# Chunked recurrent attention with a routed feed-forward: the chunk loop written out as one list, the triangular inverse taken in two halves, copies cut to their live columns

## The chip, the cores and the metric

One core of a Trainium2 chip runs the whole program. The metric is the device time in microseconds (us) of one execution; lower is better. The kernel before was run three times.

The core has a tensor engine (PE, with its weight loads shown as PEld), a vector engine (DVE), a scalar engine (ACT), GpSimd (POOL) and a queue engine (SP) that here only issues DMAs. Each takes its instructions in the order in which they were written into its queue, and waits at an instruction until the semaphores that it names are there.

## The reference, cut to what matters

```
B, H, S, D = 4, 8, 768, 40                       # r, k, v, w, a, b: each [B, H, S, D]
for t in range(S):
    y[:, :, t] = einsum('bhd,bhde->bhe', rt, state)
    Sa = einsum('bhde,bhe->bhd', state, at)
    state = state * wt[:, :, None, :] - einsum('bhd,bhe->bhde', Sa, bt) + einsum('bhd,bhe->bhde', vt, kt)

x = y.transpose(0, 2, 1, 3).reshape(3072, 320)
logits = x @ w_gate                              # [320, 8]: one of 8 experts for each token
gate_w = softmax(logits)[expert_idx]             # expert_idx = argmax
out[mask_e] = gate_w * (relu(x[mask_e] @ w1[e]) @ w2[e])      # w1 [320, 1024], w2 [1024, 320]
```

So there are 32 independent recurrences (4 batches by 8 heads) of 768 steps on a 40x40 state, then a feed-forward in which each of 3072 tokens goes through one expert.

## The kernel before

**Attention.** The 768 steps are cut into 24 chunks of 32 (`NC`, `C`). In one chunk the 32 recurrences are handled together, as four groups of eight (two "types" `ty` by two halves `j`), one group to a quarter of the 128 partitions. A chunk c goes through these stages, named by the letters that the issue order uses:

- *preparation*, up to nine chunks ahead: loads of the chunk's W, KB and A; `scan` (running product of w, DVE, L224); `inv` (1/product as Ln and Exp, ACT, L229 and L230); `gmul` (one Newton step for the reciprocal, two DVE operations, L241 and L242); `kbmul` and `qmul` (two products over 128x1024 elements, on POOL in the loop, L235 and L246);
- *E* (`estage`): 16 products on PE for the chunk's four 32x32 triangular blocks per recurrence; `m2` copies one part into `M2c`, `m1` the other back into Q (ACT, L263, L275, L276), and `m1_mask` masks it on POOL (L281);
- *inversion* (`tops`), once for a group of four chunks: 128 triangular 32x32 matrices, one to a partition, are inverted by back substitution on DVE. `step(j)` for j = 30 to 1 is a product (L301) and a subtraction (L303) on j x (31-j) elements. The first group alone does it in halves: `step2(j)` for j = 14 to 1 (L309, L311) inverts the two 16x16 diagonal blocks at once;
- `tbd`: four copies on ACT (L331) set the chunk's inverses into a block-diagonal 128x128 tile `TBD`; in the first group the corner between the two halves is made by two sets of PE products (L337, L347) instead;
- the recurrence: *R* (`rhs`, 32 PE products per chunk, one ACT copy), *U* (`ustage`, 32 products with `TBD`, four ACT copies into `SVS`), *S* (`sstage`, 32 products, then four DVE products, L408, which give the state `SVR` of the next chunk). R of the next chunk waits for them;
- beside it *T* (`sT`), *u* (`ut`), *K* (`kbt`): transposes on PE, copied by ACT; *A* (`astage`, masked by DVE, L444) and *y* (`ystage`, L463 on PE, L469 on DVE): the output;
- every second chunk *r* (`route_a`) and *b* (`route_b`): the gate, the token's expert and its row, and two indirect DMAs by POOL (L538) that scatter 128 rows each to `Xs` in memory.

One fp32 PE product is two rows of the profile, except for transposes.

**Order.** Up to chunk 4 the order is a hand-written list (`START`), kept as written on all five engines. From there on a chunk's stages are *written* in the order of the string `ORDER`, with shares of `tops` between them, and the framework's scheduler places them on the engines. Beside the stages the kernel issues products on constant data only to keep the tensor engine's clock up (`w` in `START`, and `busy`).

**Feed-forward** (`moe`). Each expert gathers its rows from `Xs` (L830), splits them and its weights into a high and a low half, and multiplies high by high, high by low and low by high: `l1` (L877 to L882), `l2` (L897 to L905), then a scaled copy and an indirect DMA to the output (L911). `check` and three operations at the end (L954 to L956) verify that w lies in a range; a product at the very end (L1065) turns that into a flag that every engine reads.

Of the kernel before, what the change touches and what calls it, by code (L numbers as in the profile page):

```python
# [42 lines left out]
START = ("W0 s0 l0 j0 W1 s1 a1 a0 w22 c0 k1 w12 l1 g0 Q0 g1 W2 s2 l2 q1 W3 s3 w9 c5 g2 a2 q2 l3 e0 w3 n0 e1 k2 w1 W4 "  # L43
# [18 lines left out]
NKB, NG = 9, 10  # L62


def prepare(inputs):
# [7 lines left out]
    W = np.zeros((NC, 80, 16, C + 1), f32)  # L73
    W[..., 1:] = em(w)
# [4 lines left out]
    VR[..., 0:40], VR[..., 64:104] = V[..., 0::2, :], V[..., 1::2, :]  # L79
# [36 lines left out]
    d["cq"] = np.broadcast_to((ii[None] == (jj % C)[:, None])[:, None, 0:16], (128, 8, 16)).astype(f32)  # L116
# [7 lines left out]
def attention(tc, nc, d, ctx, Xs, okt, sent):  # L124
# [963 lines left out]
```

## Time and profile before

| | us |
|---|---|
| three runs | 706.08, 705.46, 701.49; median 705.46 |
| the profiled execution: its time | 701.49 |
| its span, first to last instruction | 701.5 |
| first state product of the loop (L408) | starts at 71.9 |
| last state product (L408) | starts at 432.7 |
| first gather of the feed-forward | starts at 459.0 |
| busy in the span: PE, DVE, ACT, POOL | 601.3, 535.8, 422.9, 228.7 |

The profiled execution is the fastest of the three, 0.6% under the median. All times in a profile are counted from the span's start. A group's row gives its count, its busy time, the mean of one instruction in nanoseconds, and the idle time of the engine just before. PEclk is the share of its full clock that the tensor engine was granted.

### The profile page before, as it was taken

How to read it: one execution, taken by the hardware profiler on the slowest of the kernel's cores; microseconds unless marked ns; L12 is line 12 of the kernel's file. 1: busy time of each engine (PE TensorE's matmuls, PEld its weight loads, DVE VectorE, ACT ScalarE, POOL GpSimd, SP SyncE). 2: the span in 40 equal slices, each digit the busy share in tenths (PEclk: the TensorE clock that was granted, in tenths of full speed). 3: DMA queues.
4: the chain of work that ended last, by engine and by line, in shares of the span. 5: the costliest groups of instructions: out<-in, count | busy, mean ns of one | idle time of the engine just before them, and what ended most of it. 6: DMA issues, size and time to landing. Idle time of an engine off the chain costs nothing. (4 is left out here: it accounts for less than half of the span.)

```text
span 701.5 us, 25718 instructions
## 1 busy us (share of the span) xinstructions
PE 601.3 (86%) x10942; PEld 510.3 (73%) x10942; DVE 535.8 (76%) x1074; ACT 422.9 (60%) x962; POOL 228.7 (33%) x239
## 2 busy tenths in 40 slices
PE   7477786877978877868889899889999999999994
PEld 3345565766867676757778788758898898988984
DVE  7999699998999999999789634558657576485531
ACT  2565755678759867978786887445535445355320
POOL 5860534546545544457312101200111101201101
PEclk9788767897877788888889989869999999999998
DMA  6484457253434343424224332886454464552100
GB/s 200 119 210 121 141 180 254 75 161 111 123 103 121 103 122 103 133 90 129 78 82 128 111 93 82 243 245 212 134 174 127 145 220 129 168 189 74 56 1 31
DMA packets 48207, 93.26 MB, mean 133 GB/s; under 512 B 11577, under 2 KB 28090, under 8 KB 48024
## 3 DMA queue, kind: packets, MB, share of 16 engines
q1 hardware_dynamic: 45528, 83.65, 39.9%
q0 software_dynamic: 2560, 7.92, 3.2%
q8 instruction: 88, 1.44, 0.9%
q14 instruction: 31, 0.25, 0.1%
HBM read 78.98 MB, written 13.21 MB: 131 GB/s over the span
## 5 line engine op out<-in xcount | busy, mean ns | idle before, releaser
L911 POOL DMA_INDIRECT out<-yo,tok x32 | 30.8, 964 | 207.6 <-DVE yo L910 149.8
L301 DVE TENSOR_TENSOR tmp<-Mt,Tt 128x30 f32<-128x30 f32 (+9 forms) x150 | 79.7, 532 | 2.8
L303 DVE TENSOR_TENSOR Tt<-Tt,tmp 128x30 f32<-128x30 f32 (+9 forms) x150 | 77.1, 514 | 3.2
L886 DVE SCALAR_TENSOR_TENSOR hx<-m_hp,hx 128x384 fp32r<-128x384 f32 (+1 forms) x128 | 41.0, 383 | 34.9 <-ACT hx L884 34.9
L246 POOL TENSOR_TENSOR Q<-AT,G 128x1024 f32<-128x1024 f32 x18 | 50.3, 2796 | 40.9 <-DVE G L242 14.0
L884 ACT ACTIVATE hx<-m_hp 128x448 fp32r<-128x448 f32 x64 | 31.4, 543 | 49.0 <-PE m_hp L882 44.8
L897 PE MATMUL m_yp<-w2h,hx 128*128 128x320 f32 x192 | 61.0, 317 | 0.0
L899 PE MATMUL m_yp<-w2h,hx 128*128 128x320 f32 x192 | 59.1, 308 | 0.0
L898 PE MATMUL m_yp<-w2l,hx 128*128 128x320 f32 x192 | 59.1, 308 | 0.0
L402 PE MATMUL ps_r<-SVS,KS 128*40 128x40 f32 x1472 | 49.8, 228 | 9.3 <-ACT SVS L390 6.2
L364 ACT COPY KS<-ps_g 64x416 f32<-64x416 f32 x96 | 48.1, 501 | 14.8 <-PE ps_g L360 10.0
L281 POOL TENSOR_SCALAR_AFFINE_SELECT Q<-Q 32x512 f32<-32x512 f32 x44 | 38.1, 865 | 57.4 <-ACT Q L275 50.1
L255 PE MATMUL ps_g<-Q,KB 128*64 128x64 f32 x768 | 38.4, 273 | 20.9 <-POOL Q L246 10.5
L463 PE MATMUL psY<-Y,KS 128*40 128x32 f32 x1504 | 50.4, 221 | 5.2 <-DVE Y L444 4.3
L402 PEld LDWEIGHTS ps_r<-SVS,KS 128*40 128x40 f32 x1472 | 44.1, 141 | 12.3 <-ACT SVS L390 8.6
L255 PEld LDWEIGHTS ps_g<-Q,KB 128*64 128x64 f32 x768 | 34.4, 183 | 25.5 <-POOL Q L246 11.9
L331 ACT COPY TBD<-Tc 32x256 f32<-32x256 f32 x80 | 50.8, 635 | 3.2 <-DVE Tc L314 1.3
L463 PEld LDWEIGHTS psY<-Y,KS 128*40 128x40 f32 x1504 | 44.9, 142 | 10.0 <-DVE Y L444 6.7
L408 DVE TENSOR_TENSOR SVR<-ps_r,F 40x320 f32<-40x320 f32 x92 | 44.9, 488 | 8.8 <-PE ps_r L402 6.2
L877 PE MATMUL m_hp<-x,w1h 128*128 128x448 f32 x128 | 50.1, 391 | 0.4 <-ACT x L860 0.4
L538 POOL DMA_INDIRECT Xs<-xr,si x24 | 27.9, 1164 | 61.5 <-ACT TBD L331 15.9
L878 PE MATMUL m_hp<-x,w1h 128*128 128x448 f32 x128 | 47.7, 373 | 0.0
(187 smaller groups left out, 1555.2 us busy)
## 6 DMA issues: line engine op xcount, KB each, us to landing
w2r<-in_w SPq DMA_DIRECT2D x8, 1280.0 KB
w1r<-in_w SPq DMA_DIRECT2D x8, 1024.0 KB
VU<-in_VT SPq DMA_DIRECT2D x48, 160.0 KB
SVR<-in_VR SPq DMA_DIRECT2D x48, 104.0 KB
SVS<-in_VS SPq DMA_DIRECT2D x24, 208.0 KB
KB<-in_KB SPq DMA_DIRECT2D x30, 160.0 KB
KB<-in_KBP SPq DMA_DIRECT2D x9, 512.0 KB
Xs<-xr SPq DMA_DIRECT2D x7, 648.0 KB
```

The source lines that it names most:

```text
L246: eng.tensor_tensor(at(Q, s), buf(s)[3], g, ALU.mult)
L255: TE.matmul(e[j][:, x], kb[:, p, :], q[:, :, p, :], start=True, stop=True, tile_position=(0, 64 * j))
L301: V.tensor_tensor(t, Mt[:, 0:j, j:j + 1].broadcast_to([128, j, n]), Tt[:, j:j + 1, j + 1:32].broadcast_to([128, j, n]), ALU.mult)
L303: V.tensor_tensor(Tt[:, 0:j, j + 1:32], Tt[:, 0:j, j + 1:32], t, ALU.subtract)
L331: A.copy(o[bb:bb + 32, :, bb:bb + 32], t[bb:bb + 32, :, n0:n0 + 8].rearrange("p i n->p n i"))
L364: A.copy(ks[0:64, u * 8 + z:u * 8 + 8:2], ts[u][64 * z:64 * z + 64])
L402: TE.matmul(s[TR[ty], x], ks[:, p, o:o + 40], sv[:, p, o:o + 40], start=True, stop=True, tile_position=(0, o))
L463: TE.matmul(py[TR[ty], p], ks[:, p, o:o + 40], y2[:, ty, p, :], start=True, stop=True, tile_position=(0, o))
L877: TE.matmul(hp, w1h[:, k, s], xh[:, k], start=k == 0, stop=False)
L897: TE.matmul(yp, hh[:, ft, qs], w2h[:, ft], start=ft == 0, stop=False)
L898: TE.matmul(yp, hh[:, ft, qs], w2l[:, ft], start=False, stop=False)
L899: TE.matmul(yp, hl[:, ft, qs], w2h[:, ft], start=False, stop=ft == 7)
```

## The change

**Order.** `ORDER` becomes one list of some 700 words for the whole loop, chunk 0 to 23, kept as written on all five engines: a word names a stage and its chunk, and each time it comes the stage's next part is issued; `t` is one step of the inversion, `f` two products on constant data ("filler pair", twelve in all). `START` is shorter. The products of `YW` before y go, except for the last chunk; `w` in `START` falls from 140 to 85.

**Inversion.** All six groups do the 14 steps on two 16x16 halves; `step` works in place on `Tt` (no `Mt`, no mask product; POOL zeroes the half that isn't wanted with memsets, L300 to L303). `merge` makes the corner for every chunk: 32 products on 32x32 tiles, four copies, 16 products of two heads on 64x64 tiles, one copy. `TBD` and its copies go: U reads the inverses from `Tc` directly.

**Preparation.** `inv` and `gmul` go. Instead a reciprocal of 16 columns and a second scan, running backwards, give 1/product. `kbmul` and `qmul` run on DVE for all chunks.

**Recurrence and copies.** R takes both types in one product: 16 products on 64 columns by 80 instead of 32 on 32 columns by 40; its copy is 128x640 instead of 128x320. S ends in two DVE products on 40x640 instead of four on 40x320. The copies of K leave out 24 of 104 columns.

**Scatters and end.** The four scatters of two routings no longer wait for each other; nor do those of the output. In the feed-forward `x3` and its copy go (the low half of w1's last 64 rows is multiplied with both halves of x), the last expert does its short block before its last full one, and the flag is made before that block.

```diff
-ORDER = ".05 R A T U b E .2 S .2 y C u K r .5 p 2 B"
+ORDER = ("y0 B0 B1 B0 M3 B0 j4 q4 i0 A0 B1 K0 B0 U0 B1 U0 S0 u0 p5 p5 S0 M2 p6 p6 K0 i1 E5 B2 u0 B1 T1 E5 p7 R1 p7 p8  "
...
+         "R23 u22 R23 r22 r20 U23 A23 A23 T23 U23 u23 y23 r22 T23 u23 y23 ")
+TAIL = "R A T U b E S y u K r"
-YW = tuple((c < 16) + (c == NC - 1) + 5 * (c in (5, 11, 17)) for c in range(NC))
+YW = tuple(int(c == NC - 1) for c in range(NC))
     def scan(s):
-        w, f = buf(s)[:2]
-        V.tensor_tensor_scan(f.rearrange("p a b->p (a b)"), w.rearrange("p a b->p (a b)"), scn,
-                             0.0, ALU.mult, ALU.max)
-    def inv(s):
-        _, f, nt, _ = buf(s)
-        A.activation(nt, f[:, :, 1:], AF.Ln)
-        A.activation(nt, nt, AF.Exp, scale=-1.0)
+        w, f, _ = buf(s)
+        back = lambda x: bass.AP(x.tensor, x.offset + 528, [x.ap[0], [-1, 528]])
+        V.tensor_tensor_scan(f.rearrange("p a b->p (a b)"), w[:, 0:528], scn, 0.0, ALU.mult, ALU.max)
+        V.reciprocal(RC[:, 33:WN:33], f[:, :, 32])
+        V.tensor_tensor_scan(back(at(G, s)), back(w), back(RC), 0.0, ALU.mult, ALU.max)
-    def gmul(s):
-        V.tensor_tensor(g, f[:, :, 1:], nt, ALU.mult)
-        V.scalar_tensor_tensor(g, g, 2.0, nt, ALU.subtract, ALU.mult, reverse0=True)
     def tops(k):
         def first():
-            V.transpose(flat(Mt), M2c[0].rearrange("p n t->p t n"))
+            V.transpose(flat(Tt), M2c[0].rearrange("p n t->p t n"))
+            A.copy(at(ML, k)[:, 0:32], M2c[0][:, :, 0:16])
+            G_.memset(Tt[:, 0:16, 16:32], 0.0)
+            for h in (16, 8, 4, 2, 1):
+                G_.memset(bass.AP(Tt.tensor, Tt[:, h, 0:1].offset, [Tt.ap[0], [66 * h, 16 // h], [32, h], [1, h]]), 0.0)
+            G_.memset(flat(Tt)[:, 0:1024:33], -1.0)
-        def step(j):
-            n = 31 - j
-            t = tmp[:, :j * n].rearrange("p (a b)->p a b", b=n)
+        def step(j):
             n = 15 - j
             t = tmp[:, :2 * j * n].rearrange("p (h a b)->p h a b", a=j, b=n)
+    def merge(c):
...
+        q = g4([128, 8, 32])
+                TE.matmul(q[b, x], m[b, (n0 + x) * 16:(n0 + x) * 16 + 32], Tc2[b, :, h:h + 2].rearrange("p a n->p n a"),
+        for b in quads:
+            A.copy(Q1[b, :, o:o + 16].rearrange("p (h l) a->p h l a", l=2), mine(q[b], 16))
+        z = g4([128, 8, 64])
+            for b in (slice(0, 64), slice(64, 128)):
+                TE.matmul(z[b, x], Q1[b, x], t[b, h:h + 2].rearrange("p n a->p (n a)"), start=True, stop=True,
+        A.copy(t[:, n0:n0 + 8, 0:16].rearrange("p (h l) a->p h l a", l=2), mine(z, 32))
     def rhs(c):
-                TE.matmul(r[32 * bb:32 * bb + 32, h], q[:, ty, p, :], sr[:, ty, p // 2, p % 2 * 64:p % 2 * 64 + 40],
-        A.copy(rs, r)
+                TE.matmul(psS[64 * j:64 * j + 64, h, 0:80], q[:, p].rearrange("e t i->e (t i)"),
+                          sr[:, :, h, j * 64:j * 64 + 40], start=True, stop=True, tile_position=(0, 64 * j))
+        A.copy(rs, psS[:, :, 0:80])
     def ustage(c):
-                TE.matmul(u[bb:bb + 32, h], tb[:, h, bb:bb + 32], rs[:, h, :],
-                          start=True, stop=True, tile_position=(0, bb))
+                TE.matmul(u[bb:bb + 32, h], t[bb:bb + 32, c % 4 * 8 + h, :], rs[bb:bb + 32, h, bb // 32 % 2 * 40:bb // 32 % 2 * 40 + 40],
+                          start=True, stop=True, tile_position=(bb, bb))
+    def step_prep(s):
+            scan(s)
+                load_w(s + 1)
+            kbmul(s, V)
+            qmul(s, V)
+                load_a(s + 1)
```

The first place is DVE's queue near the end of an inversion. In the kernel before (`Mt`, `Tt`, `tmp` are the inversion's tiles, L532 belongs to the routing, L444 to A, L314 is the transposition that ends it):

```order
L301 TENSOR_TENSOR tmp<-Mt,Tt 128x108
L444 TENSOR_TENSOR Y_104<-ps_g,mask 64x2x256 x2
L532 RECIPROCAL xr<-gt 128x2
L303 TENSOR_TENSOR Tt<-Tt,tmp 128x4x27
L301 TENSOR_TENSOR tmp<-Mt,Tt 128x84
L303 TENSOR_TENSOR Tt<-Tt,tmp 128x3x28
L301 TENSOR_TENSOR tmp<-Mt,Tt 128x58
L303 TENSOR_TENSOR Tt<-Tt,tmp 128x2x29
L301 TENSOR_TENSOR tmp<-Mt,Tt 128x30
L303 TENSOR_TENSOR Tt<-Tt,tmp 128x30
L314 STREAM_TRANSPOSE Tc<-Tt 128x1024
```

In the changed kernel, at the start of the third group's inversion (L244 and L246 are the two scans of a preparation, the scans being printed under the name of a related operation; L253 and L258 its two products; L310 and L312 an inversion step; L397 the state products):

```order
L244 SCALAR_TENSOR_TENSOR FF<-Wt,scn 128x528
L245 RECIPROCAL RC<-FF 128x16
L246 SCALAR_TENSOR_TENSOR G_91<-Wt,RC 128x528
L310 TENSOR_TENSOR tmp<-Tt 128x28
L312 TENSOR_TENSOR Tt<-Tt,tmp 128x2x14
L253 TENSOR_TENSOR KB_87<-KB_87,FF 128x1024
L258 TENSOR_TENSOR Q_88<-AT,G_91 128x1024
L310 TENSOR_TENSOR tmp<-Tt 128x52
L312 TENSOR_TENSOR Tt<-Tt,tmp 128x2x13x2
L397 TENSOR_TENSOR SVR<-psS,F_113 40x8x2x40 x2
```

Thirty pairs to a group have become fourteen, and the preparation's two big products stand among them on the same engine.

The second place is POOL's queue in the middle of the loop. Before (L246 and L235 are the big products, L236 the small copy of the scan's last column, L281 the masks, L538 the scatters, L514 the token numbers):

```order
L246 TENSOR_TENSOR Q_76<-AT,G_93 128x1024
L538 DMA Xs<-xr,si 3584x324
L235 TENSOR_TENSOR KB_77<-KB_77,FF 128x1024
L236 COPY F_112<-FF 128x16
L281 AFFINE_SELECT Q_76<-Q_76 32x512 x2
L514 COPY xr<-cg 128x2
```

And in the changed kernel (L302 and L303 clear parts of the inversion's tile, L254 is the small copy, L293 the masks, L530 the scatters):

```order
L302 MEMSET Tt 128x16
L303 MEMSET Tt 128x32
L254 COPY F_113<-FF 128x16 x2
L503 COPY gt<-cg 128x8
L504 TENSOR_TENSOR gt<-cg,gt 128x8
L505 TENSOR_TENSOR cg<-gt 128x8
L506 COPY xr<-cg 128x2
L507 MEMSET xr 128x2x2
L293 AFFINE_SELECT Q_76<-Q_76 32x16x32 x2
L530 DMA Xs<-xr,si 3584x324 x2
```

The big products are gone from POOL; small copies, masks, memsets and scatters remain.

The third place is PE's queue over about one chunk late in the loop. Before, from R to S (L375 is R, L441 A, L415 T, L385 U, L463 y, L255 E, L402 S; six constant products of L448 stand ahead of L463 and are printed here with their first pair only):

```order
L375 MATMUL ps_r<-SVR,Q_86 32x40 x32
L441 MATMUL ps_g<-RT,VU 64x2x32 x16
L415 MATMUL ps_g<-ident,SVR 104x40 x16
L385 MATMUL ps_r<-rs,TBD 32x40 x32
L448 LDWEIGHTS scn
L448 MATMUL psY<-scn 128x512
```

And in the changed kernel from one S to the next (L392 S, L414 u, L343 the corner's second set, L355 K, L430 A, L368 R, L404 T, L378 U, L472 the gate, L447 y):

```order
L392 MATMUL psS<-SVS,KS_123 40x40 x32
L414 MATMUL ps_g<-ident,SVS 104x32 x16
L343 MATMUL ps_g<-Tc_116,NB 64x64 x16
L355 MATMUL ps_g<-ident,KB_89 128x104 x8
L430 MATMUL ps_g<-RT,VU 64x2x32 x16
L368 MATMUL psS<-SVR,Q_90 64x80 x16
L404 MATMUL ps_g<-ident,SVR 104x40 x16
L378 MATMUL psU<-RS,Tc_116 32x40 x32
L472 MATMUL ps_g<-xT,wg 32x128 x8
L447 MATMUL psY<-Y_105,KS_123 40x32 x32
L355 MATMUL ps_g<-ident,KB_73 128x104 x8
L392 MATMUL psS<-SVS,KS_123 40x40 x32
```

R has half as many rows, each wider, and the corner's two sets (L332, elsewhere, and L343) now run in every chunk.

More of the change, by code (lines that the diff above doesn't have):

```diff
@@ L315, in last @@
-            if k < 1:
-                V.transpose(flat(Tc2), Tt.rearrange("p a b->p b a")[:, 16:32])
-        o = [(1.2, first), (1.2, second)]
-        for j in range(14 if k < 1 else 30, 0, -1):
-            if k < 1:
-                o.append((2 * (0.075 + 2 * j * (15 - j) / 960), lambda j=j: step2(j)))
-            else:
-                o.append((2 * (0.075 + j * (31 - j) / 960), lambda j=j: step(j)))
-        o.append((1.2, last))
-        return o
-    def tbd(c):
-        t, n0, o = Tc[0], (c % 4) * 8, at(TBD, c)
-        if c >= 4:
-            for bb in range(0, 128, 32):
-                A.copy(o[bb:bb + 32, :, bb:bb + 32], t[bb:bb + 32, :, n0:n0 + 8].rearrange("p i n->p n i"))
-            return
+            V.transpose(flat(Tc2), Tt.rearrange("p a b->p b a")[:, 16:32])
@@ L333, in tbd, with mine @@
+            V.transpose(at(Tc, k).rearrange("p n a->p a n"), flat(Tt))
+        return [(2, first)] + [(2 * (0.12 + 2 * j * (15 - j) / 960), lambda j=j: step(j)) for j in range(14, 0, -1)] + [
+            (3.1, last)]
+    def mine(x, w):
+        return bass.AP(x.tensor, x.offset, [x.ap[0], [4 * w, 4], [3 * w, 2], [1, 16]])
+    def merge(c):
+        t, m, n0 = at(Tc, c // 4), flat(at(ML, c // 4)), c % 4 * 8
         quads = [slice(bb, bb + 32) for bb in range(0, 128, 32)]
-        q = g4([128, 8, 16])
+        q = g4([128, 8, 32])
@@ L348, in tbd @@
                           tile_position=(b.start, b.start))
         yield
-        for b in quads:
-            A.copy(o[b, :, b.start:b.start + 16], z[b])
+        A.copy(t[:, n0:n0 + 8, 0:16].rearrange("p (h l) a->p h l a", l=2), mine(z, 32))
     def kbt(c):
@@ L596, in step_u, with step_e @@
             yield from ustage(i)
[L598 to L605 removed]
+    def step_e(s):
         if s < NC:
@@ L777, in attention @@
-    for _ in step_route_b(NC):
-        pass
-    for i in range(1, 4):
-        for j in range(i + 1, 5):
-            tc.declare_no_dep(sent[-i].ins, sent[-j].ins, reason="they write different rows")
-        tc.add_manual_dep(sent[-i].ins, sent[-5].ins.name, mybir.DependencyInfo(
-            mybir.DependencyClass.Sync, mybir.DependencyReason.DATA))
+                    for t in ML:
+                        G_.memset(flat(t)[:, 512:544], 0.0)
+                    DMA.dma_start(Q1, d["cq"])
+    once = {"j": lambda s: kbmul(s, V), "q": lambda s: qmul(s, V), "M": m1_mask}
@@ new lines, in attention @@
+    groups, to, gens = iter(range(1, NC // 4)), [], {}
+    for op in ORDER.split():
+        if op == "t":
+            if not to:
+                to = tops(next(groups))
+            to.pop(0)[1]()
+            continue
+        if op == "f":
+            hot = g4([128, 512])
+            for _ in range(2):
+                TE.matmul(hot, scn[:, 0:128], scn[:, 0:512], start=True, stop=True)
+            continue
+        if op[0] in once:
+            once[op[0]](int(op[1:]))
+            continue
+        if op not in gens:
+            gens[op] = steps[op[0]](int(op[1:]))
+        next(gens[op], None)
@@ new lines, in attention @@
+    gens = {}
+    manual.__exit__(None, None, None)
+    for i in (NC, NC + 1):
+        with tc.manual_schedule(engines={mybir.EngineType.PE}):
+            for step in TAIL.split():
+                if step == "b":
+                    for _ in gens.pop("r", ()):
+                        pass
+                elif step == "r" and i == NC:
+                    gens["r"] = step_route(i)
+                    for _ in range(3):
+                        next(gens["r"])
+                elif step != "r":
+                    for _ in steps[step](i):
+                        pass
@@ L785, in attention @@
+    for g in range(0, len(sent), 4):
+        for i in range(g, g + 4):
+            for j in range(g, i):
+                tc.declare_no_dep(sent[i].ins, sent[j].ins, reason="they write different rows")
+            for j in range(max(g - 4, 0), g) if i > g else ():
+                tc.add_manual_dep(sent[i].ins, sent[j].ins.name, mybir.DependencyInfo(
+                    mybir.DependencyClass.Sync, mybir.DependencyReason.DATA))
     cnt, oh = g4([128, 8]), held["oh"]
```

334 lines of the change are left out of this document (131 added, 203 removed), and 30 rows, old and new, of tables (ORDER, START).

## The prediction

> **What bounds the kernel now.** I read the busy time by stage first, then the starts of one operation that comes once a chunk, then the groups by shape, then the timeline. The stretches show (columns: PE, PEld, DVE, ACT, POOL busy us with counts, granted clock, DMA share, GB/s):
>
> ```profile
> 160.00:200.00 40.00, 31.44 (x819) 27.17 (x817) 37.27 (x73) 30.75 (x73) 22.26 (x21) 0.80 0.38 116
> 240.00:280.00 40.00, 30.38 (x880) 27.53 (x869) 37.63 (x81) 28.87 (x69) 19.35 (x22) 0.82 0.39 114
> 371.00:396.00 25.00, 23.71 (x781) 20.54 (x776) 21.84 (x65) 18.25 (x44) 3.89 (x10) 1.00 0.37 112
> 490.00:694.00 204.00, 201.75 (x1178) 178.66 (x1176) 122.78 (x262) 84.91 (x183) 29.62 (x31) 1.00 0.39 126
> ```
>
> In the middle of the loop DVE is busy 93% of the time and PE 78%: DVE bounds it. Late (371 to 396), when preparations have run out, PE is busy 95%. From 490 on PE is full and nothing here changes its work. The span splits at four events:
>
> ```profile
> L408 DVE TENSOR_TENSOR SVR<-ps_r,F x92: 481/489/495, 71.9 to 432.7; 40x320 f32<-40x320 f32 x92
> 454.10 4.07 DMA Xs<-xr,si
> 459.00 3.40 DMA xg<-Xs
> ```
>
> 92 state products are 23 chunks of four: start to 71.9; loop 71.9 to 432.7, 360.8 for 22 intervals, 16.4 each; 26.3 from there over the last chunk and its scatter to the first gather at 459.0; 242.5 of feed-forward and end. Sum 701.5, the profiled execution's own time; the median of the three runs, 705.46, is 4.0 more.
>
> Why DVE takes 16.4:
>
> ```profile
> L301 DVE TENSOR_TENSOR tmp<-Mt,Tt 128x30 f32<-128x30 f32 (+9 forms) x150 | 79.7, 532 | 2.8
> L303 DVE TENSOR_TENSOR Tt<-Tt,tmp 128x30 f32<-128x30 f32 (+9 forms) x150 | 77.1, 514 | 3.2
> L309 DVE TENSOR_TENSOR tmp<-Mt,Tt x14: 161/246/754, 44.3 to 57.7; 128x28 f32<-128x28 f32 x2, 128x52 f32<-128x52 f32 x2, 128x72 f32<-128x72 f32 x2, 128x88 f32<-128x88 f32 x2
> L311 DVE TENSOR_TENSOR Tt<-Tt,tmp x14: 200/256/2378, 44.5 to 57.9; 128x28 f32<-128x28 f32 x2, 128x52 f32<-128x52 f32 x2, 128x72 f32<-128x72 f32 x2, 128x88 f32<-128x88 f32 x2
> 256.58 0.40 DVE L303 TENSOR_TENSOR Tt<-Tt,tmp 128x234 f32<-128x234 f32 x1
> 257.32 2.39 POOL L246 TENSOR_TENSOR Q<-AT,G 128x1024 f32<-128x1024 f32 x1
> 257.44 2.53 DVE L303 TENSOR_TENSOR Tt<-Tt,tmp 128x228 f32<-128x228 f32 x1
> ```
>
> The inversion's pairs take 156.8 us for five groups, 7.8 a chunk. And part of that is waiting: the same operation on fewer elements takes 2.53 instead of 0.40 when a big POOL product runs.
>
> **The change on DVE.** Prices for what it adds or keeps:
>
> ```profile
> 26.06 1.25 DVE L224 TENSOR_TENSOR_SCAN KB<-Q,scn 128x528 f32<-128x528 f32 x1
> L235 DVE TENSOR_TENSOR KB<-KB,FF 128x1024 f32<-128x1024 f32 x2 | 2.4, 1222 | 1.8 <-DMA KB<-in_KBP 1.8
> L246 DVE TENSOR_TENSOR Q<-AT,G 128x1024 f32<-128x1024 f32 x2 | 2.4, 1202 | 0.0
> L286 DVE STREAM_TRANSPOSE Mt<-M2c 128x1024 f32<-128x1024 f32 x6 | 11.8, 1963 | 6.9 <-ACT M2c L263 6.9
> L314 DVE STREAM_TRANSPOSE Tc<-Tt 128x1024 f32<-128x1024 f32 x6 | 7.5, 1242 | 0.2
> L847 DVE TENSOR_TENSOR w2l<-w2r,w2h 128x640 fp32r<-128x640 f32 x4 | 3.0, 820 | 0.0
> L444 DVE TENSOR_TENSOR Y<-ps_g,mask 64x512 f32<-64x512 f32 x48 | 32.6, 681 | 11.4 <-PE ps_g L441 10.8
> ```
>
> A preparation is two scans at 1.25, a small reciprocal (0.16 by the routing's) and products of 1.22 and 1.20: 5.1. An inversion is 14 x (0.246 + 0.256) = 7.0, and transpositions of 1.96, about 1.0 (half the size) and 1.24: 11.2, or 2.8 a chunk. State products: two at 0.82 (the 640-element row), 1.6. A 1.4, y 0.7, routing some 0.9. Sum **12.5** a chunk. The backward scan is in no row: I take the forward one's 1.25; the other end is the 1.96 that a strided transposition takes against 1.24, which would make DVE 13.2. A gain below 1.25 is not to be had from the same 528 elements. The last transposition writes with a stride now: 1.24 to 1.96, 0.2 a chunk at most.
>
> POOL keeps masks, small copies, scatters and new memsets. What they do to DVE:
>
> ```profile
> 25.20 2.87 POOL L722 MEMSET SVR<- 128x3328 f32 x1
> 49.46 3.05 POOL L281 TENSOR_SCALAR_AFFINE_SELECT Q<-Q 32x512 f32<-32x512 f32 x4
> 50.32 0.74 DVE L311 TENSOR_TENSOR Tt<-Tt,tmp 128x100 f32<-128x100 f32 x1
> ```
>
> Under the memset the scan of 26.06 above took its usual 1.25, so I cost the memsets at nothing but their wait (six small ones, some 1 us a group, inside the inversion). Under the masks an operation of 100 elements took 0.74, against a median of 0.256: some 0.5 for each of the two masks of a chunk, up to 1.0, DVE 13.5 at worst. [...]
>
> **The change on ACT.**
>
> ```profile
> L331 ACT COPY TBD<-Tc 32x256 f32<-32x256 f32 x80 | 50.8, 635 | 3.2 <-DVE Tc L314 1.3 <-PE ps_r L385 0.2
> L229 ACT ACTIVATE nt<-FF 128x512 f32<-128x512 f32 x20 | 12.7, 633 | 14.2 <-DVE FF L224 14.0
> L351 ACT COPY TBD<-ps_g 32x128 f32<-32x128 f32 x16 | 4.1, 257 | 7.8 <-PE ps_g L347 7.6
> L364 ACT COPY KS<-ps_g 64x416 f32<-64x416 f32 x96 | 48.1, 501 | 14.8 <-PE ps_g L360 10.0
> L390 ACT COPY SVS<-ps_r 32x320 f32<-32x320 f32 x96 | 40.1, 418 | 6.1 <-PE ps_r L385 3.9
> L846 ACT CAST w2h<-w2r 128x640 fp32r<-128x640 f32 x4 | 2.6, 731 | 0.0
> ```
>
> A chunk loses four copies of 0.635 and Ln and Exp at 0.63 each, 3.8; it gains five corner copies at about 0.26, 1.3, and 0.3 where R's copy goes from 0.43 to 0.73; K's four copies go to the 320-element price, -0.3. From about 14 a chunk to 11.5. ACT is not the bound.
>
> **The change on PE.** One late chunk at full clock, stage by stage:
>
> ```profile
> 383.90 1.42 PE L402 MATMUL ps_r<-SVS,KS 128*40 128x40 f32 x60 [0.17 <-ACT SVS L390]
> 385.25 1.00 PE L425 MATMUL ps_g<-ident,SVS 32*104 32x32 f32 x16
> 386.19 0.93 PE L360 MATMUL ps_g<-ident,KB 104*128 104x104 f32 x8
> 390.00 1.15 PE L441 MATMUL ps_g<-RT,VU 128*64 128x64 f32 x32
> 391.09 0.83 PE L415 MATMUL ps_g<-ident,SVR 40*104 40x40 f32 x16
> 391.85 0.80 PE L385 MATMUL ps_r<-rs,TBD 128*32 128x40 f32 x64
> 60.39 0.74 PE L337 MATMUL ps_g<-Tc,ML 32*32 32x16 f32 x64 [3.31 <-DVE Tc L316]
> 63.30 1.05 PE L347 MATMUL ps_g<-Tc,NB 32*32 32x16 f32 x64
> 236.69 1.98 PE L441 MATMUL ps_g<-RT,VU 128*64 128x64 f32 x32
> ```
>
> S 1.4, u 1.0, K 0.9, A 1.15, T 0.8, U 0.8; R has U's form (0.8), y has S's (1.4); the routing's small products I put at 1.5 a chunk, an estimate from six stages of 0.4 to 0.6 every second chunk. Sum 9.8 without E; E has A's form, 1.15. The state products of that chunk and the next lie 10.7 apart in the timeline, 1.09 times the sum.
>
> In the changed kernel R is 32 rows of A's form, 1.15 (+0.35); the corner's first set 0.74; its second, 32 rows of two-head tiles, lies between 0.74 and A's 1.15, and I take 1.15; fillers 0.2. So 12.3 without E and **13.4** with it. U's tiles change at the same row count: no cost. Thus PE is the longest of three near-equal engines (13.4, 12.5, 11.5), and moving work off DVE beyond 13 buys nothing more.
>
> **The sum.** Start: DVE's work before the first state product is 4.3 until the first scan, four preparations (20.4), the fifth's scans (2.7), a masked copy set (1.7), the inversion (11.2), and 7.5 of further preparations: 47.8; with waits for loads I take 52, against 71.9. First interval: four preparations stand ahead of the second state product, 23.4; with load waits 25. Then 15 intervals with E and 6 without. The late stage's factor 1.09 held 5% of PE idle, part of it behind ACT's copies that go; I take 1.065: 15 x 14.3 + 6 x 13.1 = 293. The recurrence alone (R, copy 0.73, U, four copies 1.7, S, products 1.6: 7.4) fits inside. Last chunk 26.3, unchanged. Feed-forward 242.5: K=128 products for `w1l` replace pairs of half ones at the same stage time, `x3`'s copies lie under a full PE, and the last block's chain loses one operation of about half a microsecond, the flag another half: 241.5. Total 52 + 25 + 293 + 26.3 + 241.5 = **638**.
>
> The independent scatters shorten POOL's waits, which end no chain but the last, where the last four were independent already: nothing.
>
> **Rivals.**
>
> *The engines do not mesh* (0.18). The list is fixed, so a copy or product that is late holds what stands behind it. A scan waits for POOL's small copy of the last one's column (L254), and that stands behind masks, which wait for ACT. Against it: each queue has work of other chunks between. Intervals of 15.8 and 14.0 give 52 + 25 + 237 + 84 + 268 = 666.
>
> *The engines mesh fully* (0.12). Factor 1.0 and the corner's second set at 0.74: 13.0 and 11.9 give 52 + 23 + 195 + 71 + 268 = 609.
>
> *The start does not move* (0.06): loads, not DVE, set it, since the first 120 us moved 166 to 195 GB/s. Then 72 instead of 52, about 658.
>
> *The clock falls: slower* (0.04). Most of the constant products go. In a stretch with the clock low, A's stage took 1.98 instead of 1.15. If S, y, A, E, R, U and the corner are all slow, a chunk's PE time grows by some 5.4 us (0.6, 0.6, 0.83, 0.85, 0.8, 0.5, 1.2). Intervals of 17.0 undo the gain: that is 48% of the time slow, a granted clock of 0.76. At 0.70 the intervals are 17.7 and 16.2 and the time 708. The middle of the kernel before had 0.80 with PE 78% busy; the stretch with PE 95% busy had 1.00, and a fuller PE is what the forecast needs anyway. [...]
>
> *It does not do what it says* is small here: the instruction lists show fourteen pairs and no big POOL product.
>
> **The numbers.** The forecast has 0.60, with 620 to 655 of its own (factor 1.0 to 1.12, the backward scan within its bounds). The range reaches to the first two rivals: 608 to 672. What a measurement of this kernel tells from no change is about 1%. Faster by more: 0.60 + 0.18 + 0.12 + 0.06 less a little, 0.92; same 0.04; slower 0.04.
>
> **What would show it.** Right: first state product near 52, last near 370; in the middle DVE, PE and ACT all busy at 80 to 92%, clock 0.9 or more; inversion operations at medians near 0.25 with none of 2 us; first gather near 397. Wrong: state products 16 apart with DVE waiting for PE or POOL; clock under 0.8; backward scans well over 1.25; the first state product past 60.

## The result, and the profile after

| | before | after |
|---|---|---|
| runs, us | 706.08, 705.46, 701.49, 702.18 | 650.80, 645.33, 647.76, 648.91 |
| median | 703.82 | 648.34 |
| ratio | | 0.9251 (95% interval 0.9190 to 0.9313) |
| profiled execution: time, span | 701.49, 701.5 | 650.80, 649.1 |

The time fell by 55 us, 7.5%; the forecast was 638, with 608 to 672 around it. The profile after is of the slowest of the four runs, that before of the fastest. Some executions of a kernel run over 1.5% longer than its fastest; the ratios below leave those out, the medians do not.

The span splits at the same events as before: the state product (now L397, two to a chunk), the last scatter of the attention, the first gather. The group's row (ns, first and last start in us):

```profile
L397 DVE TENSOR_TENSOR SVR<-psS,F x46: 815/822/828, 52.4 to 386.7; 40x640 f32<-40x640 f32 x46
```

and the chain that ended last (start, us, what):

```profile
410.69 2.75 DMA Xs<-xr,si
...
414.44 3.04 DMA xg<-Xs
```

| stage, us | before | predicted | after |
|---|---|---|---|
| start to first state product | 71.9 | 52 | 52.4 |
| first interval (to the second chunk's product) | 21.1 | 25 | 31.3 |
| the other 21, to the last product | 339.7 | 293 | 303.0 |
| last chunk, to the first gather | 26.3 | 26.3 | 27.7 |
| feed-forward and end | 242.5 | 241.5 | 234.7 |
| sum | 701.5 | 638 | 649.1 |

The 21 intervals (columns: span, then PE, PEld, DVE, ACT, POOL busy us with counts, granted clock, DMA share, GB/s), of the kernel before and of the changed one:

```profile
93.00:432.70 339.70, 282.43 (x8047) 247.37 (x8048) 297.82 (x620) 258.09 (x593) 143.05 (x152) 0.83 0.40 119
```

```profile
83.70:386.70 303.00, 277.16 (x9093) 251.46 (x9107) 222.61 (x437) 221.07 (x597) 70.39 (x153) 0.97 0.44 128
```

DVE lost 75 us and is 73% busy; PE is 91% busy. PE ran 1046 rows more than before (the corners bring 2048, R has 672 fewer), in 5 us less: the clock went from 0.83 to 0.97.

On DVE, the pieces that were priced (least, median and longest ns):

```profile
L310 DVE TENSOR_TENSOR tmp<-Tt x84: 173/250/769, 32.2 to 335.4; 128x28 f32<-128x28 f32 x12, 128x52 f32<-128x52 f32 x12, 128x72 f32<-128x72 f32 x12, 128x88 f32<-128x88 f32 x12
...
L246 DVE TENSOR_TENSOR_SCAN G<-Wt,RC x21: 1257/1258/1769, 6.0 to 302.9; 128x528 f32<-128x528 f32 x21
...
L253 DVE TENSOR_TENSOR KB<-KB,FF x21: 1192/1215/1655, 7.1 to 304.0; 128x1024 f32<-128x1024 f32 x21
...
L316 DVE STREAM_TRANSPOSE Tc<-Tt 128x1024 f32<-128x1024 f32 x6 | 11.6, 1932 | 0.0
```

The backward scan costs what the forward one does (1.258), the strided transposition 1.93, an inversion step 0.25 with none above 0.77 (0.81 for the subtraction). The 1.77 and 1.66 are scans and products under a POOL mask (the chain of the first interval, below, shows two).

What PE waits for in the 21 intervals, longest groups (engine, waiting line, releaser: total us, times, longest):

```profile
PE psY L447 <- issue: 7.1, 6, 1.5
PE ps_g L343 <- issue: 2.6, 4, 1.0
PE ps_g L520 <- issue: 1.6, 1, 1.6
```

"issue" means that no semaphore is seen. Most of these stops fall in the middle of a stage. One of them, in the timeline of PE (start, us, operation):

```profile
108.89 0.49 PE L447 MATMUL psY<-Y,KS 128*40 128x32 f32 x15
110.77 0.42 PE L447 MATMUL psY<-Y,KS 128*40 128x32 f32 x13 [1.39 <-issue]
```

After 15 rows of a y whose 64 rows wait for one thing, PE does nothing for 1.39 us. There are 21 such stops of 0.3 us or more in the loop, 17.9 us in all. (One of them is missing in the 20 and 16.5 us that an expectation below names.) Counted in PE's instructions (products, weight loads, semaphores), from one to the next are 257, 255, 256, 256, 256, 513, 765, 768, 1022, 255, 1536, 1536, ... : always a multiple of 256, but for one or two. The DMA queue that carries instructions moved 96 packets in the span, of 16 KB each; PE's 24,099 instructions are 94 blocks of 256:

```profile
q8 instruction: 96, 1.57, 1.0%
```

At each of the 21 stops PE resumes 2.2 to 2.9 us after the last of these packets began. I took it that PE had run out of instructions; the experiments measure how they arrive.

### The profile page after: what moved, and what is told of

Read it like the earlier page. It is cut to its first block, busy times and chain, and to the rows that moved or that the text cites. A ratio compares the mean times of both kernels' runs of the same rounds, so it can differ in the third digit from the quotient of the medians.

```text
span 649.1 us, 27374 instructions
## 1 busy us (share of the span) xinstructions
PE 580.2 (89%) x11887; PEld 520.9 (80%) x11904; DVE 455.5 (70%) x880; ACT 365.5 (56%) x912; POOL 129.8 (20%) x236
## 4 chain that ended last, share of the span: by engine, by line
PE 71%; DVE 11%; issue 7%; ACT 4%; DMA 4%; SPq 1%; POOL 0%; POOLq 0%; DVEq 0%; ACTq 0%
PE psY L447 4%; PE m_hp L847 4%; PE m_yp L866 4%; PE m_yp L867 4%; PE m_yp L868 4%; PE psS L392 4%; PE m_hp L848 4%; PE m_hp L849 4%; PE ps_g L343 4%; PE ps_g L430 4%; PE psS L368 3%; PE ps_g L332 3%; PE ps_g L414 3%; PE ps_g L355 2%; PE psU L378 2%
## 5 line engine op out<-in xcount | busy, mean ns | idle before, releaser
L397 DVE TENSOR_TENSOR SVR<-psS,F 40x640 f32<-40x640 f32 x46 | 37.8, 822 | 28.6 <-PE psS L392 26.9
L293 POOL TENSOR_SCALAR_AFFINE_SELECT Q<-Q 32x512 f32<-32x512 f32 x46 | 40.8, 887 | 71.9 <-ACT Q L288 60.2
L275 ACT COPY M2c<-ps_g 32x256 f32<-32x256 f32 x96 | 35.0, 364 | 32.5 <-PE ps_g L267 31.3
L433 DVE TENSOR_TENSOR Y<-ps_g,mask 64x512 f32<-64x512 f32 x48 | 32.9, 686 | 26.9 <-PE ps_g L430 26.4
L847 PE MATMUL m_hp<-x,w1h 128*128 128x448 f32 x128 | 47.8, 374 | 0.4 <-ACT x L831 0.4
L849 PE MATMUL m_hp<-x,w1l 128*128 128x448 f32 x128 | 47.3, 369 | 0.0
L267 PE MATMUL ps_g<-Q,KB 128*64 128x64 f32 x768 | 29.8, 236 | 17.9 <-issue 10.9
L359 ACT COPY KS<-ps_g 64x320 f32<-64x320 f32 x96 | 40.4, 421 | 9.2 <-PE ps_g L355 5.4
L383 ACT COPY SVS<-psU 32x320 f32<-32x320 f32 x96 | 40.1, 418 | 6.9 <-PE psU L378 4.9
L267 PEld LDWEIGHTS ps_g<-Q,KB 128*64 128x64 f32 x768 | 26.8, 149 | 21.1 <-issue 12.1
L447 PE MATMUL psY<-Y,KS 128*40 128x32 f32 x1504 | 36.2, 205 | 7.6 <-issue 7.1
L408 ACT COPY KS<-ps_g 40x320 f32<-40x320 f32 x92 | 38.6, 420 | 7.2 <-PE ps_g L404 5.7
L447 PEld LDWEIGHTS psY<-Y,KS 128*40 128x40 f32 x1504 | 32.9, 124 | 10.7 <-issue 8.6
L392 PE MATMUL psS<-SVS,KS 128*40 128x40 f32 x1472 | 37.2, 214 | 1.6 <-issue 1.1
L530 POOL DMA_INDIRECT Xs<-xr,si x24 | 25.1, 1046 | 64.2 <-ACT KS L359 12.5
```

Source lines behind the costliest of these rows:

```text
L267: TE.matmul(e[j][:, x], kb[:, p, :], q[:, p], start=True, stop=True, tile_position=(0, 64 * j))
L293: G_.affine_select(q[o:o + 32, :, ty], q[o:o + 32, :, ty], pattern=[[0, 16], [-1, 32]], base=0, channel_multiplier=1, compare_op=ALU.is_gt ...
L359: A.copy(halves(ks[0:64, u * 8 + z:u * 8 + 8:2]), halves(ts[u][64 * z:64 * z + 64]))
L392: TE.matmul(psS[TR[ty], h, j * 40:j * 40 + 40], ks[:, p, o:o + 40], sv[:, p, o:o + 40], start=True, stop=True, tile_position=(0, o))
L447: TE.matmul(py[TR[ty], p], ks[:, p, o:o + 40], y2[:, ty, p, :], start=True, stop=True, tile_position=(0, o))
L847: TE.matmul(hp, w1h[:, k, s], xh[:, k], start=k == 0, stop=False)
```

## The experiments

The chips. The first four kernels below (doubled stages and long products) ran together on one chip; the first form of the trains, the halves, the feed-forward's edit and y with 16 products on a second; the second form of the trains, the unwritten order, no fillers and the second buffer on a third; each time with the kernel before beside them (medians 704.31, 703.83, 704.90). The changed kernel itself was not among them; two of these kernels are the same as it up to the last expert and serve instead; each was executed once.

**A issued twice; DVE's mask of A twice; ACT's copies of T twice; long products ahead of A.** The edits:

```diff
+                    for _ in range(2):      # e1, around A's product;  e2: around its masked copy;  e3: around T's copy
```
```diff
+        hot = g4([128, 512])                # e4, ahead of A
+        for _ in range(3):
+            TE.matmul(hot, scn[:, 0:128], scn[:, 0:512], start=True, stop=True)
```

> The changed kernel with every product of stage A issued twice: 768 more rows on PE, 31.4 us of its busy time, nothing on the other engines, and A is not on the way from one state to the next. Theory (the prediction's: PE is what the loop is filled with): the whole cost shows, 31 us at no idle to 34 at the loop's present ratio of 1.09 between interval and busy time, so 679 to 683 from the changed kernel's 648.3. Rival (the engines wait for each other along the recurrence and PE has room): under 12 us, below 660.

> The changed kernel with DVE's masked copy of A (L433, 0.686 us) done twice: 48 more instructions, 32.9 us of DVE, about the size of the run with A doubled. Theory (PE bounds the loop; DVE was busy 222.6 of its 303 us): it goes into DVE's idle time but for places where DVE is full (the first interval has none of it), 0 to 8 us, 648 to 656. Rival (DVE and PE are tied, as the prediction's sums of 12.5 and 13.4 almost are, so that each engine's order holds the other): 16 us or more, 664 and above. Rival (DVE still bounds): 33 us, 681.

> The changed kernel with ACT's copies of T (L408, 0.420 us) done twice: 92 more instructions, 38.6 us of ACT, which was busy 221.1 of the loop's 303 us. Theory (PE bounds): 0 to 10 us, 648 to 658; a little more than on DVE, since SVS and RS copies of the recurrence stand in the same queue. Rival (ACT's queue holds the recurrence): 20 us or more, 668 and above.

> The changed kernel with three products on constants of 512 columns ahead of each A: 72 long products of about 0.37 us at full clock, 26.6 us of PE time, but only some 144 instructions against 1536 in the run with A doubled. Theory as the prediction had it (PE's time counts, whatever it is made of): 27 to 29 us, about 676. Rival, from the trace of the changed kernel: PE stops in the middle of a stage, with no wait, at 20 places that lie exactly 256 of its instructions apart or multiples of that, 16.5 us in all, so that part of the loop is bound by how fast its instructions arrive; then long products that bring few instructions run while the next block arrives, and a third or so of those stops goes: 18 to 23 us, about 669.

| | median | ratio to before | loop of 21 | stops in it |
|---|---|---|---|---|
| A twice | 671.7 | 0.9544 (0.9458 to 0.9629) | 325.7 | 23, 19.1 us |
| DVE's mask twice | 670.1 | 0.9555 (0.9460 to 0.9651) | 311.9 | 14, 12.1 us |
| ACT's copies twice | 667.1 | 0.9477 (0.9404 to 0.9550) | | |
| long products | 656.4 | 0.9318 (0.9234 to 0.9402) | 308.7 | 7, 7.2 us |

The loops of A twice, of the long products and (over 0.5 us more than the loop) of the doubled mask:

```profile
83.90:409.60 325.70, 299.01 (x9766) 273.56 (x9780) 222.44 (x437) 221.26 (x597) 71.06 (x153) 0.96 0.40 120
```

```profile
85.30:394.00 308.70, 289.62 (x9113) 255.51 (x9144) 222.48 (x437) 220.50 (x597) 70.44 (x153) 0.96 0.43 126
```

```profile
85.60:398.00 312.40, 283.03 (x9099) 256.91 (x9105) 252.35 (x479) 220.75 (x597) 72.32 (x153) 0.93 0.42 124
```

and the long products ahead of one A, in PE's timeline:

```profile
150.17 0.82 PE L425 MATMUL ps_g<-scn 128*128 128x512 bf16 x2
...
150.92 1.15 PE L433 MATMUL ps_g<-RT,VU 128*64 128x64 f32 x32
```

My price for A was the busy time of its group, that of the long products their rows' durations; both count the overlap of one row with the next, where the start-to-start distance counts. A's 32 rows take 1.15 us from the first start to the last end, of which 0.23 is the last row: 0.92 for a second A, 19 us over the loop's 21 chunks. Measured: 22.7 more in the loop, all of it. The three long products take from 150.17 to A's first row at 150.92 (one of the three is missing in the trace): 0.75, 15.8 us over the 21 chunks. Measured: 5.7 more in the loop, a third. The difference is the stops: 23 remain where 1536 instructions were added, 7 where 144 were. 15.8 us less the 10.7 of stops that went is 5.1. The two ran side by side, and A twice is 15.3 slower, with 9 us more of PE's busy time in the loop.

The doubled mask and copies cost more than the "0 to 8" and "0 to 10" that I gave to engines with a quarter of their time idle: 22 and 19 us by the medians, 17 and 20 from fastest run to fastest. That lies between the theory and the rival in which the fixed order ties the engines. In the profile of the doubled mask DVE has 30 us more work in the loop, and the loop is 9 us longer: most of that work did go into DVE's idle time. How much of the rest is order and how much a chip on which the changed kernel was not run, these runs do not separate; against the long products, on the same chip, the two are 11 to 14 us slower.

**The arrival of instructions by itself.** Trains of products on constants behind the last expert. First with the products one below the other on the same columns, then in turn on the left and the right ones. The second form's edit (the first has 512 products, the wider ones 64 by 64, and three experts' loads):

```diff
+        for i in range(640):
+            o = 64 * (i % 2)
+            TE.matmul(q[o:o + 40, 0:32], ident[:, 0:40], ident[:, 0:32], ..., tile_position=(0, o))
+        ...                                    # the same with 64 by 96; six experts' loads; both again
```

> The changed kernel with four trains of products on constants behind its last expert, which nobody reads: 512 fp32 products with 32 columns (1024 rows of the profile, 2048 instructions with their weight loads, 8 blocks of 256), 512 with 64 columns, then three experts' weights are loaded again and the same two trains run under the loads. Theory (a block of 256 instructions cannot follow the one before it sooner than about 3.85 us): a train with 32 columns takes 8 times 3.85, 31 us, with a stop of about 1 us at every block; with 64 columns a block takes 4.6 us at the 36 ns that A's rows take and has no stop, 37 us. Under the loads the stops are longer, if the loads are what delays a block. Rival (the stops in the loop come from waits that the trace does not show): 1024 times the 21 ns of S's and y's rows, 21.5 us, without stops.

> The changed kernel with four trains behind its last expert again, now with products on the left and right half of the columns in turn, as S and y have them: 640 fp32 products with 40 by 32 (1280 rows, 2560 instructions, 10 blocks of 256), 640 with 64 by 96, then six experts' weights are loaded and the same two trains run under the loads. Theory (a block of 256 instructions of PE cannot follow the one before sooner than about 3.85 us): the first train takes 38.5 us, 21 ns a row with a stop of about 1.1 us in every block; the second, at 40 ns a row or more, has blocks above 5 us and no stops; under the loads the first has longer stops. Rival (the stops have another cause): the first takes 27 us with no stop.

In the first form, a train in PE's timeline:

```profile
657.82 39.19 PE L946 MATMUL m_hp<-mident 128*40 128x32 f32 x1018
```

A row took 38 ns instead of 21, a block 4.9 us, and no stop came without loads: not dense enough to test the limit. The second form:

```profile
674.17 2.64 PE L947 MATMUL m_hp<-mident 128*40 128x32 f32 x128 [0.65 <-issue]
677.92 2.64 PE L947 MATMUL m_hp<-mident 128*40 128x32 f32 x128 [1.10 <-issue]
681.66 2.65 PE L947 MATMUL m_hp<-mident 128*40 128x32 f32 x128 [1.10 <-issue]
```

and its four trains by stretch:

```profile
666.30:701.00 34.70, 26.14 (x1272) 25.11 (x1274) 0.00 (x0) 0.53 (x1) 0.97 (x1) 1.00 0.03 9
702.00:754.00 52.00, 52.00 (x1265) 52.00 (x1261) 0.00 (x0) 0.00 (x0) 0.00 (x0) 1.00 0.01 3
762.00:815.90 53.90, 37.86 (x1206) 36.72 (x1204) 0.00 (x0) 0.00 (x0) 0.00 (x0) 0.63 0.87 271
816.00:869.00 53.00, 53.00 (x1265) 53.00 (x1264) 0.00 (x0) 0.00 (x0) 0.00 (x0) 0.98 0.01 3
```

128 rows (256 instructions), a stop of 1.10, 128 rows, a stop of 1.10: a block every 3.745 us with no other DMA. With wider products (41 ns a row, 5.3 us a block) nothing stops. Under the experts' loads (DMA 87% busy) the first train takes over 54 us instead of 35, with stops up to 2.9 us and a granted clock of 0.63 instead of 1.00. The loads had ended when the second wide train began. The expected 38.5 for the first was 35: its first blocks came faster, and 3.745 stands for 3.85. The rival's 27 without stops is out.

So over many blocks of short products PE got 256 instructions in about 3.75 us and no more. Fewer can come faster, as if some blocks stood ready: in the changed kernel's loop 256 instructions once passed within 1.7 us, but no 2048 within less than 29.8, 3.72 a block. At 3.745 the loop's 71 blocks need some 266 us, of 303. S, y, U and the corner's first set issue a weight load and its product in 9 to 20 ns, where the train's limit is 29 (3.745 us for 128 pairs).

**The halves alone in the kernel before.** All groups take the 14 pairs, every chunk makes its corner. The rest is the kernel before, but for R's copy and the inversion's working tile, which are smaller or single, and the 14 pairs, which stand at every second place of the 30.

```diff
-            if k < 1:                                   # in tops: the halves for the first group only
+            if True:
-        if c >= 4:                                      # in tbd: four copies instead of the corner
-            ...
```

> The kernel before with one part of the change alone: all groups invert in two halves with 14 pairs, and every chunk makes its corner with the kernel before's two sets of 32 products (its order, its preparation and its copies else unchanged; the working tile of the inversion and R's copy are smaller or single, to make room for a second copy of the left columns). Theory by the prediction's prices: DVE loses 4.8 us a chunk and gains four small copies, some 1.0, so 12.5; PE, which took 13.45 a chunk with the clock at 0.83, gains 1.8 and becomes the bound at 15.2; intervals of about 15.4 instead of 16.4 over some 19 chunks, 20 us less, 684 against 704. Rival (DVE was all of it): 3.8 a chunk, 70 us less, 634. Rival (the order sets the pace, and no part alone gains): 700 to 708.

758.4 us, ratio 1.0742 (1.0639 to 1.0845): slower by 54, which no theory had. Its 21 intervals:

```profile
90.90:485.30 394.40, 329.42 (x10509) 291.58 (x10524) 243.86 (x548) 234.78 (x612) 136.65 (x152) 0.76 0.35 104
```

DVE is freed (62% busy), by 2.6 us a chunk where 3.8 were priced. But PE, with 2462 more rows, has its clock at 0.76, down from 0.83, and takes 47 us more busy time, of the 55 that the loop is longer. My term "PE becomes the bound at 15.2" used the clock of the kernel before. What the single buffers cost was not measured apart; no wait for R's copy stands among PE's longest.

**The changed kernel without the written order.** The list sets only the order of writing; behind `START` the scheduler places the instructions.

```diff
+    manual.__exit__(None, None, None)          # ahead of the loop over ORDER instead of behind it
```

> The changed kernel with all its parts, but with the 715 words only setting the order in which the stages are written; behind START the framework's scheduler places them on the engines, as in the kernel before. Theory (the parts free DVE, and only an order that keeps PE fed turns that into time; the halves put alone into the kernel before left PE at a granted clock of 0.72 in the loop and cost 54 us): PE's rows are spread out, the clock in the loop falls to 0.75 to 0.85, and the time is 690 to 750. Rival (the parts make the gain whatever the order): 645 to 665.

769.1 us, ratio 1.0943 (1.0883 to 1.1002), above even the expected 690 to 750. The loop:

```profile
113.30:505.40 392.10, 322.17 (x8960) 291.50 (x8976) 213.34 (x429) 218.38 (x587) 62.29 (x145) 0.80 0.30 88
```

PE's longest wait in it, and one of DVE's:

```profile
PE psS L368 <- DVE SVR L397: 16.1, 6, 4.0
```

```profile
DVE KB L253 <- DMA KB<-in_KB: 44.1, 10, 8.2
```

Nearly the same instructions, with DVE 54% and ACT 56% busy, take 89 us more in the loop (64 more than in the one profile of the changed kernel's loop on that chip, below): DVE waits for loads, PE waits for the state, and the clock is at 0.80. Placed by the scheduler, the same parts are slower than the kernel before. The other half of the comparison, the written order with the kernel before's parts, was not run.

**The feed-forward's edit alone in the kernel before.**

```diff
+            TE.matmul(hp, w1l[:, 2, s], x2[:, 0], start=False, stop=True)
-        for r, hp, s, x in zip((slice(0, 64), slice(64, 128)), hps, fs, (x2, x3)):
-            TE.matmul(hp, w1l[r, 2, s], x[r, 0], start=False, stop=True)
```

> The kernel before with the feed-forward's two edits alone: x3 and its copy gone, and w1's low last rows multiplied over all 128 rows. By the traces a pair of half products took 404 ns plus 95 ns more before it and up to 18 ns in the next product, the two full ones take 2 times 203: 0.4 to 0.7 us an expert and eight experts, 3 to 6 us less, 698 to 701 against 704. Rival (the prediction's: the same stage time): no difference.

697.1 us, ratio 0.9917 (0.9876 to 0.9957), 5.8 us less, as expected. The pair in the kernel before's timeline:

```profile
526.51 0.37 PE L880 MATMUL m_hp<-x,w1h 128*128 128x448 f32 x1
526.81 0.47 PE L882 MATMUL m_hp<-x,w1l 64*128 64x448 f32 x2
527.21 0.47 PE L877 MATMUL m_hp<-x,w1h 128*128 128x448 f32 x1
527.52 0.36 PE L878 MATMUL m_hp<-x,w1h 128*128 128x448 f32 x1
```

Between full products the distance is 0.20. Into the pair it is 0.30, the pair holds PE for 0.40, and the product after it for 0.31: 1.01 where four full ones need 0.81. Four times an expert, that is 0.8.

**y with 16 products.**

```diff
+            for p in range(16):
+                TE.matmul(zs[p // 8][0:104, p % 8], ks[:, p, :], y2[:, :, p, :], start=True, stop=True)
```

> The changed kernel with y taken as R is: 16 products on 104 columns by 64 instead of 32 on 40 columns by 32, so 64 instructions of PE fewer in each of 23 chunks (PE rows of y 64 to 32, about 1.35 to 1.15 us), paid with four copies of 64 or 40 by 256 on DVE instead of one of 104 by 512 (0.42 each by the rows of the last chunk, so 1.0 us a chunk more) and one more accumulator from the ring of four. Theory (the instructions' arrival holds PE): 0.25 block a chunk, about 0.96 us less there, 22 us over the loop where it is held throughout, half of that where it is not: 10 to 20 us less, 628 to 638. Rival (PE's time counts): 5 us less. Rival (DVE is tied with PE): the 23 us of DVE cost what the doubled masks did, two thirds, so 15 us more, 663.

697.3 us, where 628 to 638 was expected (runs from 686.1 to 700.8); the loop takes 343.6 against 321.5 in the first form of the trains, on the same chip. The eight products of a half (16 rows) take 1.4 us between their first and last start, so y takes 2.8, where 64 rows on two column halves take 1.28 (medians over the loop). The narrow products on the left and right columns run beside each other, as the trains show (21 ns a row against 38 on the same columns); a wide one takes 92 ns a row. PE's busy time in the loop is 32 us longer, DVE's 22. With y priced so wrongly, the run says nothing on the supply.

**No fillers; a second buffer for w.**

```diff
-         "R2 p10 B3 R2 T2 f i4 t t U2 T2 ...   # e10: the twelve words f are left out
+         "R2 p10 B3 R2 T2 i4 t t U2 T2 ...
+    Wt = [T("Wt", [128, WN]), T("Wt1", [128, WN])]     # e11: loaded two chunks ahead; and i0 to i3 behind i6
```

> The changed kernel without its twelve pairs of constant products in the loop (24 products of 0.37 us, 8.9 us of PE, and 48 instructions). Theory: PE has that much room between stages, as the run with 72 long products showed (8 us for 26.6), so 3 us less at most, 645 to 649, if the clock stays; the clock was low after stretches with PE waiting, and twelve pairs in 300 us are too few to hold it. Rival (they hold the clock up): the granted clock of the loop falls from 0.97 to below 0.93, and the time is 655 or more. Rival (PE's time is the bound): 9 us less, 639.

> The changed kernel with a second buffer for w, loaded two chunks ahead, and with the first four of the seven fills of Xs (648 KB each, between 42 and 85 us) moved behind the last of the seven. It is aimed at the first interval, 31.3 us where the prediction had 25: DVE waits there 5.5 us for w, while the DMA engines are 72% busy. Theory: 4 to 6 us less in that interval and nothing after it, 642 to 645. Rival (the masks on POOL, which stretch scans and products from 1.26 to 1.7 us, and PE behind them set that interval): under 2 us, 646 to 650. Rival (the fills collide with the loads of the next chunks instead): 648 or more.

672.7 us (ratio 0.9529, 0.9453 to 0.9606) and 665.9 (0.9474, 0.9423 to 0.9526), against 648.3 in the result. Their loops do not lay that to the edits. The second form of the trains, whose loop is the changed kernel's instruction for instruction, ran beside them:

```profile
84.60:412.70 328.10, 295.47 (x9064) 266.11 (x9074) 222.67 (x437) 221.10 (x597) 72.53 (x153) 0.90 0.41 118
55.50:84.60 29.10, 18.04 (x536) 17.11 (x535) 25.33 (x25) 18.04 (x48) 7.01 (x10) 0.74 0.59 185
```

328.1 there in its one execution, and its last scatter of the output at 667.1 instead of 641.0; the loops without fillers and with the second buffer took 327.5 and 330.1, in one profile each. Neither edit shows a difference in the loop. The second buffer's first interval was 27.4 against 29.1 there and 31.3 in the changed kernel's profile. Neither is shown to be better or worse than the changed kernel.

## Why the prediction was right, and where it was wrong

*The start* (52): right, 52.4. DVE's work set it (47.9 us busy, 47.8 forecast); the rival that loads do is out.

*The bound.* PE is the longest of three, as forecast. My stage prices give 16 chunks with E at 13.4 and 5 without at 12.3, 276 (the forecast counted 15 and 6); PE was busy 277.2. So close a match is partly luck: the prices are at full clock, and a granted clock of 0.97 means some 20 us of the loop at half clock (0.50 granted; 20.5 in the trace), by the prediction's two durations of A (1.98 and 1.15) an estimated 9 us of busy time that was not in the forecast. DVE came out at 10.6 a chunk instead of 12.5 in this stretch, since only 14 of the 24 preparations lie in it, so "80 to 92% busy" was wrong for DVE and ACT (73% each).

*The factor 1.065* for gaps: wrong, 303.0 / 277.2 is 1.093, 10 us. Of the 25.8 us of idle PE 17.9 are stops at blocks of instructions, a cause that was not among the terms. ACT's copies, which I had named, hold PE under 4 us.

*The first interval, "with load waits 25"*: wrong by 6. The chain through it:

```profile
59.94 2.03 DMA Wt<-in_W
...
65.28 4.36 DMA Wt<-in_W
...
71.35 1.70 DVE G L246
...
76.17 3.17 DMA AT<-in_A
...
81.94 1.71 DVE Q L258
```

Each load of w is issued when the scan has read the one buffer, and takes 2 to 4.4 us to be there; I had allowed 1.6 in all. And a scan and a product took 1.7 instead of 1.25, under masks.

*The feed-forward, "at the same stage time"*: wrong the other way, 234.7 instead of 241.5. The term took the pair to be as long as two full products, which it is (0.40), and left out the 0.10 that is lost at each of its edges; the experiment gives 5.8 of the 7.8 us. The rest lies at its two ends (first gather to first product 4.9 instead of 5.9; the last expert).

*The sum.* It came nearer than its terms: the first interval and the loop cost 16 us more than forecast, and the 7 that the feed-forward gained hide part of that.

*The clock.* Forecast 0.9 or more, measured 0.97. The rival of a falling clock came true in the two kernels without the written order, one with the halves alone and one with all parts (0.76 and 0.80). It counts slow time as half clock. That is how the clock falls here: in the traces of both kernels the granted clock is 1.00 or 0.50, in pieces of 3.41 us or whole multiples of it. The prediction's A of 1.98 us and its A of 1.15, in the kernel before:

```profile
236.69:238.67 1.98, 1.98 (x34) 1.86 (x34) 1.98 (x2) 1.31 (x4) 1.98 (x1) 0.53 0.51 148
390.00:391.15 1.15, 1.15 (x34) 1.08 (x34) 1.00 (x9) 0.70 (x3) 0.00 (x0) 1.00 0.54 165
```

In the changed kernel's loop the clock fell only behind gaps in PE. That constant products keep it up, which is what the kernel issues them for, no run shows: the loop without its fillers took 327.5 us at 0.90, the one with them on the same chip 328.1 at 0.90. Pairs of neighbouring stretches of 3.4 us in the changed kernel:

```profile
209.20:212.60 3.40, 2.17 (x74) 1.89 (x71) 3.02 (x14) 2.42 (x7) 1.89 (x2) 1.00 0.88 234
212.60:216.00 3.40, 3.39 (x84) 3.19 (x85) 1.70 (x8) 1.90 (x5) 0.90 (x2) 0.50 0.62 201
284.30:287.70 3.40, 1.83 (x38) 1.66 (x32) 2.05 (x4) 2.98 (x8) 0.00 (x0) 1.00 0.49 124
287.70:291.10 3.40, 3.40 (x130) 3.26 (x129) 1.43 (x5) 0.00 (x0) 2.16 (x3) 0.50 0.15 55
```

PE is busy 64% and 54% of one stretch, and the clock is half in the next, in which PE is full. All six times that the clock fell here between 85 and 400 us, PE had been busy 54 to 82% of the stretch ahead. The reverse does not hold: twelve other stretches with PE busy 62 to 82% were followed by full clock, like this one with 62%:

```profile
137.50:140.90 3.40, 2.10 (x71) 1.95 (x72) 3.37 (x5) 2.31 (x7) 0.00 (x0) 1.00 0.38 106
140.90:144.30 3.40, 3.25 (x89) 2.76 (x88) 2.20 (x6) 1.64 (x4) 0.00 (x0) 1.00 0.55 173
```

What else decides stays open. Four of the six hold one of the stops of 0.8 to 1.6 us, so a late block can cost its stop and then a stretch at half clock; five other stops of that size were not followed by one.

*Not settled:* why the same loop took 303.0, 321.5 and 328.1 us in profiles of the result and of the second and third chip, with a granted clock of 0.97, 0.94 and 0.90. One part can be seen. On those two chips PE also stops, with no semaphore and at no block's end, right behind POOL's indirect scatters. The second form of the trains, PE and POOL, and then PE at the same place of the changed kernel, where the same 64 rows run through behind the same scatter:

```profile
297.92 0.97 POOL L530 DMA_INDIRECT Xs<-xr,si  x1 [0.30 <-issue]
298.68 0.35 PE L332 MATMUL ps_g<-Tc,ML 32*32 32x32 f32 x6 [0.41 <-issue]
299.43 0.92 PE L332 MATMUL ps_g<-Tc,ML 32*32 32x32 f32 x46 [0.41 <-issue]
```

```profile
289.96 0.97 POOL L530 DMA_INDIRECT Xs<-xr,si  x1 [0.30 <-issue]
289.96 1.19 PE L332 MATMUL ps_g<-Tc,ML 32*32 32x32 f32 x64
```

Such stops of 0.2 us or more take 4.8 us (14) and 5.7 us (16) of the two loops, each within 2.6 us of a scatter's start; the changed kernel's profile has none. Why these chips have them was not tested, and most of the rest of the 18 and 25 us is PE's busy time, 11 and 18 us longer at the lower clock. The kernel before does not vary so (medians 703.8 to 704.9). The changed kernel itself was timed in the result alone; elsewhere its gain may be smaller.

## What to carry to other kernels

Price products by the distance between starts, never by a row's duration: that was the mistake in the prices of A twice and of the long products. Where stages have many short products, count PE's instructions too (256 in 3.75 us in the train) and put long products between dense stages. An edit that frees one engine can lose if the next engine is left with gaps: the halves alone cost 54 us, all parts placed by the scheduler 64, and the gain was seen only with the written order that keeps PE fed.

## What the runs showed of the hardware that was not expected

- PE stopped at blocks of 256 instructions: in the train one block in 3.745 us without other DMA, with stops up to 2.9 us under loads at 271 GB/s.
- All six falls to half clock (0.50 granted) between 85 and 400 us of the changed kernel came behind a stretch of 3.4 us with PE busy 54 to 82%; twelve such stretches were followed by full clock.
- Products on two column halves ran beside each other (21 ns a row in the dense train, against 38 on the same columns).
- A pair of 64-row products in the feed-forward took as long as two full ones (0.40 us), and 0.1 us more at each edge.
- On two chips PE stopped for some 0.4 us, twice, right behind an indirect scatter; in the result's profile it did not.
